# Narrower clears of the value pads, the decayed rows' pads cleared on VectorE alone, and new instruction orders in a fused linear-attention and gated feed-forward kernel

## The chip, the cores and the metric

The kernel runs on one core of one Trainium2 chip. The metric is the device time of one execution in microseconds (us); lower is better. Before the change the median of three runs is 193.56 us (193.5 to 193.87). The engines are TensorE (PE, with PEld for its weight loads), VectorE (DVE), ScalarE (ACT), GpSimd (POOL) and SyncE (SP). Loads and stores are issued from the instruction streams of SP, ACT and POOL, in the order of each stream.

## The reference

```python
# q, k, v, f_logit: (4, 8, 768, 48) = batch, heads, sequence, head size
f = 1.0 / (1.0 + np.exp(-f_logit))
for t in range(S):
    state = f[:, :, t, :, None] * state + np.einsum('bhd,bhe->bhde', k[:, :, t], v[:, :, t])
    y[:, :, t] = np.einsum('bhd,bhde->bhe', q[:, :, t], state)
x = y.transpose(0, 2, 1, 3).reshape(B * S, H * D)          # 3072 x 384
out = (np.maximum(x @ w_gate, 0.0) * (x @ w_val)) @ w_out   # 384 -> 1536 -> 384
```

A recurrence with a decay for every head and key column gives 3072 rows of 384 values; a gated feed-forward network follows.

## The kernel before

**The work.** The sequence is cut into chunks of 128 positions: 6 chunks times 4 batches give 24 blocks. Inside a block the recurrence becomes matrix products: cumulated logarithms of the decay turn into two factors, one on k and one on q (the decayed rows, tile `hats`); scores of k against q are masked and multiplied with v, and a carried state adds the past. The first 16 blocks (chunks 0 and 1) are worked two at a time as a unit of 256 positions, the rest one by one. Four blocks make one feed-forward group of 512 rows. TensorE does the matrix products of both halves, so the attention of later chunks and the feed-forward groups of earlier ones are interleaved.

**Names of operations.** The code records every operation under a short name, with chunk and block: `f`, `k`, `q`, `v` loads are `Lk0.2` (chunk 0, blocks 2 and 3), weight loads `wg0+2` (gate weights, columns 0 and 1 of 12; also `wv`, `wo`), stores `S00`. For block 0.1 the steps are
- `ef`, `ln`: ACT, exponential and logarithm of the forget logits (lines 478, 481), one pair for two blocks
- `cum01`: PE, cumulated sums (lines 494, 498; 503 and 506 in later chunks)
- `ek01`, `eq01`: ACT, exponentials of them (lines 516, 518); `dc01`: the decay of the state
- `hk01`, `hq01`: the decayed rows, k or q times an exponential (line 540 if on POOL, 541 if on DVE); both inputs and the output are in SBUF
- `tk01`, `tq01`: PE transposes of the decayed rows (line 552); `ck01`, `cq01`: their copies out of PSUM (556 DVE, 557 ACT). In chunks 2 to 5 a DMA transpose does both (line 560)
- `v01`: the cast copy of v into the padded tile `vpad` (570 POOL, 571 DVE, 572 ACT)
- `s00`: PE scores of a unit (line 650; later 584); `m000` and so on: DVE masks (657, later 592), four for a unit
- `y00`, `kv00`, `yi01`: PE, values times scores, state products, products with the old state (672, 695, 708; later 745, 756, 772); `st`, `ss`, `sd`: the state's update (450, 454, 456)
- `x01`: copy of the block's output as feed-forward input (line 597)

The feed-forward steps are `g` and `u` (gate and value products, line 792), `r` (relu, 797 ACT or 798 DVE), `p` (product, line 800, DVE), `o` (output product, line 813), `d` (copy out, 819 ACT or 820 DVE). In group 0 the first four columns are done for blocks 0 and 1 and for blocks 2 and 3 apart: `g00.2` and `g02.3` are such halves, of 256 rows instead of 512.

**Who orders it.** Nothing is scheduled when the kernel is built. `ORDER` lists for each engine the numbers of its operations in order, `BANKS` gives the PSUM bank of each product in PE's order, and `HELD` adds waits: `57: 58` makes load 57 wait for the landing of load 58. `lay_out` turns these lists into streams; `waits` puts in the semaphore waits that reads and writes ask for. A negative number in PE's list, such as `~7512`, is a row of idle-time fillers: 7 products of zeros with 512 columns (line 877).

**Pads.** A head is 48 wide. In `hats` every head has 64 columns, the last 16 zero. In `vpad` a pair of heads takes 112 columns: 48 values, 16 pad, 48 values. Products that read 32 columns at a time read the pad too (columns 32 to 63 and 48 to 79 of a pair). `fill` records such a clear as a memset.

```python
    for i in range(NH):       # 6 buffers of hats
        fill("DVE" if i < 3 else "POOL", f"hats{i}", hats[:, i, :, :, D:64], 0.0, 256, -14 + i)
    for i in range(NV):       # 6 buffers of vpad
        fill("POOL", f"vpad{i}", vpad[i][:], 0.0, VW, -8 + i)
```

Of the kernel before, what the change touches and what calls it, by code (L numbers as in the profile page):

```python
# [24 lines left out]
        45, ~60100, 76, 87, ~4512, 84, ~3512, 92, 82, 103, ~2512, 94, 123, 112, 97, ~7512, 120, ~2512, 130, 102, 128, 106,  # L25
        118, 139, 158, 133, 154, 232, 243, ~3512, 150, 152, 146, 138, 279, 268, 142, 156, 160, 148, 174, 176, 170, 172, 186,
# [13 lines left out]
    ],  # L40
    "ACT": [
# [8 lines left out]
    ],  # L50
    "DVE": [
# [25 lines left out]
}  # L77

HELD = {
    51: 53, 57: 58, 59: 63, 63: 58, 65: 69, 67: 71, 70: 50, 71: 60, 72: 54, 517: 68,  # L80
}

BANKS = [
# [158 lines left out]
def bass_hgrn2_outer__then__ffn_reglu_kernel(  # L242
# [10 lines left out]
    B, H, S, D = q.shape  # L253
# [6 lines left out]
    NP = H // 2  # L260
# [4 lines left out]
    VW, SW = NP * VSTEP, NP * SSTEP  # L265
# [7 lines left out]
    hats = sb("hats", [128, NH, 2, H, 64], BF16)  # L273
# [86 lines left out]
    for i in range(NH):  # L360
        fill("DVE" if i < 3 else "POOL", f"hats{i}", hats[:, i, :, :, D:64], 0.0, 256, -14 + i)
    for i in range(NV):
        fill("POOL", f"vpad{i}", vpad[i][:], 0.0, VW, -8 + i)
# [579 lines left out]
```

## Time and profile before

| what | value |
|---|---|
| median of three runs | 193.56 us |
| the profiled execution, its own time | 193.41 us |
| its span | 191.7 us |
| PE busy | 186.0 us, 97% of the span |
| DVE busy | 146.7 us, 77% |
| ACT busy | 83.4 us, 44% |
| POOL busy | 60.0 us, 31% |
| granted TensorE clock over the span | 1.00 |

The span runs from the first to the last instruction of one execution; its own time is 1.71 us more. Busy time is the union of an engine's instructions. The instructions of an engine overlap a little: the next one starts before the record of the one ahead ends. So the steps from start to start are shorter than the durations, and in a merged row of a timeline (a start, a length, a count) the length divided by the count is the step.

### The profile page before, as it was taken

What the parts mean: (1) busy time and instruction counts of PE and PEld (TensorE: products, weight loads), DVE (VectorE), ACT (ScalarE), POOL (GpSimd) and SP (SyncE); (2) the same over time, 40 slices, a digit from 0 to 9 for tenths busy, and PEclk for the clock granted to TensorE, in tenths of its full rate; (3) what the DMA queues carried; (4) which work ended last, traced back from release to release, by engine and by line L of the source; (5) the groups of instructions that cost most, each with busy time, mean ns of one, the idle gap of its engine ahead of it and who ended that gap; (6) DMA issues with size and microseconds to landing.
All of it is one profiled execution on the core that took longest, in us unless ns stands there. A gap on an engine that the chain in (4) does not pass through costs nothing.

```text
span 191.7 us, 4882 instructions
## 1 busy us (share of the span) xinstructions
PE 186.0 (97%) x2006; PEld 109.7 (57%) x2006; DVE 146.7 (77%) x264; ACT 83.4 (44%) x183; POOL 60.0 (31%) x92
## 2 busy tenths in 40 slices
PE   7899999999999999999999999999999999999994
PEld 7555675565645556655455755556555565555553
DVE  4469946999768989879986789996888947677331
ACT  2776963520387780472213996513351220222211
POOL 8899320201055820368200283911180000000000
DMA  5999999999989999899999999993239010000413
GB/s 149 325 285 261 206 208 278 204 225 279 241 185 193 225 212 208 160 187 255 204 162 220 238 203 236 176 202 79 64 120 180 20 41 3 2 0 0 164 44 123
DMA packets 110311, 32.44 MB, mean 169 GB/s; under 512 B 103504, under 2 KB 110032, under 8 KB 110288
## 3 DMA queue, kind: packets, MB, share of 16 engines
q1 hardware_dynamic: 95120, 25.44, 62.4%
q0 software_dynamic: 3776, 3.54, 11.4%
q10 hardware_dynamic: 11392, 3.15, 7.4%
q8 instruction: 16, 0.26, 0.6%
q14 instruction: 7, 0.06, 0.1%
HBM read 25.95 MB, written 4.72 MB: 160 GB/s over the span
## 4 chain that ended last, share of the span: by engine, by line
PE 75%; DMA 10%; DVE 5%; ACT 5%; issue 1%; POOL 1%; SPq 1%; ACTq 0%
PE ps L792 40%; PE ps L813 24%; DMA f_in<-in_f_logit_dram 7%; DMA wg<-in_moe_w_gate_dram 3%; PE ps L584 2%; DVE gT L800 2%; DVE hats L541 2%; PE ps L745 1%; PE ps L672 1%; PE ps L503 1%; POOL hats L540 1%; ACT f_in L478 1%; ACT expo L518 1%; PE ps L756 1%; ACT bneg L481 1%
## 5 line engine op out<-in xcount | busy, mean ns | idle before, releaser
L800 DVE TENSOR_TENSOR gT<-relu,ps 128x512 bf16<-128x512 bf16 (+1 forms) x76 | 48.5, 654 | 15.4 <-PE ps L792 11.4
L792 PE MATMUL ps<-xT,wg 128*128 128x512 bf16 (+1 forms) x228 | 57.8, 368 | 0.1
L792 PE MATMUL ps<-xT,wv 128*128 128x512 bf16 (+1 forms) x228 | 57.5, 368 | 0.0
L813 PE MATMUL ps<-wo,gT 128*128 128x384 bf16 (+2 forms) x300 | 51.9, 320 | 0.2 <-DVE gT L800 0.2
L797 ACT ACTIVATE relu<-ps 128x512 bf16<-128x512 f32 (+1 forms) x39 | 21.8, 565 | 46.2 <-PE ps L792 26.6
L813 PEld LDWEIGHTS ps<-wo,gT 128*128 128x128 bf16 x300 | 27.1, 98 | 18.4 <-DVE gT L800 1.2
L792 PEld LDWEIGHTS ps<-xT,wv 128*128 128x128 bf16 x228 | 23.6, 108 | 19.7 <-ACT expo L518 0.3
L792 PEld LDWEIGHTS ps<-xT,wg 128*128 128x128 bf16 x228 | 23.3, 108 | 19.1 <-DMA wg<-in_moe_w_gate_dram 0.6
L798 DVE TENSOR_SCALAR relu<-ps 128x512 bf16<-128x512 f32 (+1 forms) x37 | 24.8, 673 | 5.4 <-PE ps L792 4.4
L570 POOL CAST vpad<-v_in 128x384 bf16<-128x384 f32 x14 | 7.5, 550 | 43.6 <-PE ps L745 22.4
L592 DVE TENSOR_TENSOR ptm<-ps,tri 128x512 bf16<-128x512 f32 x32 | 19.9, 680 | 1.3 <-PE ps L584 1.3
L540 POOL TENSOR_TENSOR hats<-q_in,expo 128x384 bf16<-128x384 f32 x14 | 14.5, 1045 | 9.5 <-ACT expo L518 8.7
L478 ACT ACTIVATE f_in<-f_in 128x768 f32<-128x768 f32 x12 | 10.1, 845 | 14.1 <-DMA f_in<-in_f_logit_dram 14.0
L540 POOL TENSOR_TENSOR hats<-k_in,expo 128x384 bf16<-128x384 f32 x13 | 13.8, 1071 | 7.0 <-ACT expo L516 3.8
L456 POOL TENSOR_TENSOR st<-ssum,dec 128x384 bf16<-128x384 f32 x11 | 9.7, 878 | 16.1 <-DVE ssum L454 16.1
L518 ACT ACTIVATE expo<-ps 128x384 f32<-128x384 f32 x24 | 11.7, 492 | 4.2 <-PE ps L503 2.9
L597 ACT ACTIVATE xT<-ps 128x384 bf16<-128x384 f32 x10 | 5.4, 548 | 16.9 <-PE ps L672 8.3
L516 ACT ACTIVATE expo<-ps 128x384 f32<-128x384 f32 x24 | 11.6, 493 | 1.1 <-PE ps L494 0.6
L819 ACT ACTIVATE osb<-ps 128x384 f32<-128x384 f32 (+1 forms) x15 | 7.3, 483 | 10.3 <-PE ps L813 9.8
L657 DVE TENSOR_TENSOR ptm<-ps,tmask 128x512 bf16<-128x512 f32 x16 | 10.2, 681 | 1.2 <-PE ps L650 1.1
L877 PE MATMUL ps<-zeros 128*128 128x100 bf16 (+1 forms) x81 | 10.6, 307 | 0.0
L481 ACT ACTIVATE bneg<-f_in 128x768 bf16<-128x768 f32 x12 | 10.1, 842 | 0.2
(78 smaller groups left out, 169.8 us busy)
## 6 DMA issues: line engine op xcount, KB each, us to landing
out_dram<-osb SPq DMA_DIRECT2D x23, 192.0 KB, 2.4
f_in<-in_f_logit_dram SPq DMA_DIRECT2D x11, 384.0 KB, 5.9
k_in<-in_k_dram SPq DMA_DIRECT2D x11, 384.0 KB, 5.7
q_in<-in_q_dram SPq DMA_DIRECT2D x10, 384.0 KB, 5.7
v_in<-in_v_dram SPq DMA_DIRECT2D x8, 384.0 KB, 5.1
v_in<-in_v_dram ACTq DMA_DIRECT2D x4, 384.0 KB, 6.4
q_in<-in_q_dram ACTq DMA_DIRECT2D x2, 384.0 KB, 6.5
wg<-in_moe_w_gate_dram POOLq DMA_DIRECT2D x2, 384.0 KB, 8.8
```

The lines of the kernel that those rows point to most:

```text
L478: add(f"ef{c}{b0}", by("ACT", lambda: sc.activation(raw, raw, AF.Exp, scale=-1.0), act_(n)), keys, keys, key=P)
L481: add(f"ln{c}{b0}", by("ACT", lambda: sc.activation(bo, fl, AF.Ln, bias=1.0), act_(n)), keys + [f"bneg{bi}"], [f"bn{bi}_{x % 2}" for x in ...
L516: add(f"ek{c}{b}", by("ACT", lambda: sc.activation(ex[:, 1, :], bc.ap[:, 0:HD], AF.Exp, scale=1.0), act_(HD)), [bc], [f"expk{ei}"], key=P + 1)
L518: add(f"eq{c}{b}", by("ACT", lambda: sc.activation(ex[:, 0, :], bc.ap[:, 0:HD], AF.Exp, scale=-1.0), act_(HD)), [bc], [f"expq{ei}"], key=P ...
L540: return {**by("POOL", lambda: gp.tensor_tensor(o, i_, e_, ALU.mult), pool_(HD)), **by("DVE", lambda: ve.tensor_tensor(o, i_, e_, ALU.mult ...
L592: add(f"m{c}{b}{j}", by("DVE", lambda b=b, j=j, mi=mi: ve.tensor_tensor(ptm[mi][:, j, :, :], s[b, j].ap[:, :].rearrange("p (n t) -> p n t" ...
L792: z = te.matmul(bank.ap[:, 0:n], wt[:, kt, w_cols(j)], xT[xi][:, kt, n0:n1], start=(kt == 0), stop=(kt == NK - 1))
L797: add(f"r{c}{b0}.{j}", {**by("ACT", lambda: sc.activation(rdst, gate.ap[:, 0:n], AF.Relu), act_(n)), **by("DVE", lambda: ve.tensor_scalar_ ...
L798: **by("DVE", lambda: ve.tensor_scalar_max(rdst, gate.ap[:, 0:n], 0.0), dve_(n))}, [gate], [f"relu{ri}"], key=P)
L800: add(f"p{c}{b0}.{j}", by("DVE", lambda: ve.tensor_tensor(gT[gi][:, j, n0:n1], rdst, val.ap[:, 0:n], ALU.mult), dve_(n)), [val, f"relu{ri} ...
L813: z = te.matmul(o.ap[:, 0:e1 - e0], gT[gi][:, j, b * C:(b + 1) * C], wo[:, j, e0:e1], start=(j == 0), stop=(j == NJ - 1))
L877: te.matmul((op.opens[0].ap if op.opens else banks[7])[:, 0:fill % 1000], zeros[:, 0:128], zeros[:, 0:fill % 1000], start=True, stop=True, ...
```

## The change

The two clears read now:

```diff
     for i in range(NH):
-        fill("DVE" if i < 3 else "POOL", f"hats{i}", hats[:, i, :, :, D:64], 0.0, 256, -14 + i)
+        fill("DVE", f"hats{i}", hats[:, i, :, :, D:64], 0.0, 256, -14 + i)
     for i in range(NV):
-        fill("POOL", f"vpad{i}", vpad[i][:], 0.0, VW, -8 + i)
+
+        fill("POOL", f"vpad{i}", vpad[i][:].rearrange("p (n e) -> p n e", n=NP)[:, :, D:64], 0.0, 64, -8 + i)
```

A clear of `vpad` covers 64 columns instead of 448, and the three clears of `hats` that were on POOL are on DVE. All lists of `ORDER`, all of `BANKS`, and `HELD` are new:

```diff
 ORDER = {
     "PE": [
-        45, ~60100, 76, 87, ~4512, 84, ~3512, 92, 82, 103, ~2512, 94, 123, 112, 97, ~7512, 120, ~2512, 130, 102, 128, 106,
+        45, ~60100, 87, 76, ~7512, 94, ~2512, 84, 92, 82, 103, ~2512, 97, 112, 123, ~7512, 120, 130, 118, ~1512, 102, 128,
...
 HELD = {
-    51: 53, 57: 58, 59: 63, 63: 58, 65: 69, 67: 71, 70: 50, 71: 60, 72: 54, 517: 68,
+    57: 53, 59: 62, 63: 58, 65: 63, 66: 51, 67: 71, 70: 50, 71: 60, 806: 72,
 }
```

The same lists by name, from the first product after the opening fillers to the first gate product of blocks 2 and 3 (F4 is a row of four fillers):

```
PE before:  cum00 cum01 F4 tq00 F3 tk01 tk00 kv00 F2 tq01 cum03 cum02 s00 F7 tq02 F2 tq03 y00 tk03 yi01 tk02 kv02
            g00.3 s02 g00.2 cum10 cum11 F3 g00.1 u00.1 g00.0 y02 cum13 cum12 yi03 u00.2 u00.3 u00.0 g02.3
PE after:   cum01 cum00 F7 tq01 F2 tq00 tk01 tk00 kv00 F2 s00 cum02 cum03 F7 tq02 tq03 tk02 F1 y00 tk03 kv02 yi01
            s02 g00.2 g00.3 F1 g00.0 g00.1 u00.1 cum10 cum11 u00.3 y02 F2 yi03 u00.2 u00.0 g02.3
ACT before: ef00 ln00 eq00 dc00 ek01 eq01 ek00 ef02 ck01 ln02 ek03 v03 eq02 eq03 dc02 ek02 cq03 x00 ef10 ln10
ACT after:  ef00 ln00 v01 ek01 eq01 ek00 eq00 dc00 cq01 ef02 ck01 ln02 v02 eq02 eq03 ek02 dc02 ek03 cq02 cq03 x01 ef10
DVE before: (clears) v01 v00 hq00 cq00 hk00 ck00 st00 ss10 cq01 4 masks cq02 hk03 hk02 ck03 x01 ck02 st01
DVE after:  (clears) v00 hk01 hk00 cq00 ck00 st00 ss10 m000 m010 m001 hq03 hk02 m011 hk03 ck02 x00 ck03 st01
POOL before:(clears) wg2+2 a clear hk01 hq01 wo0+2 wv0+2 sd10 v02 hq02 hq03 wg0+2 wv2+2 wg4+4 wv4+4 wv8+4 wg8+4
POOL after: (clears) wg2+2 2 clears hq01 hq00 wo0+2 wv0+2 wg0+2 v03 sd10 hq02 wv2+2 wg4+4 wv4+4 wv8+4 wg8+4
SP before:  Lf0.0 Lq0.0 Lf0.2 Lv0.2 Lk0.2 Lf1.0 Lf1.2 Lq1.2 Lk1.0 Lq1.0 Lk1.2 Lk3.2 Lv2.2 Lq2.2 Lk2.0
SP after:   Lf0.0 Lq0.0 Lf0.2 Lv0.2 Lk0.2 Lf1.0 Lf1.2 Lq1.2 Lk1.0 Lq1.0 Lk1.2 Lq2.2 Lq2.0 Lf4.0 Lv2.2 Lf2.0
```

Holds before, by name: `wg0+2` waits for `Lk0.2`, `wv2+2` for `Lf1.0`, `Lk1.0` for `wv4+4`, `Lk1.2` for `wv8+4`, `Lk3.2` for `wg8+4`. After: `wg0+2` waits for none, `wv2+2` for `Lk0.2`, `Lq1.2` for `wg0+2`, `Lk1.0` for `wg4+4`, `Lk1.2` for `wv4+4`. `Lk3.2` has none any more, nor has `wo4+4` (it waited for `Lq0.2`), and `Lq5.2` waits for `wo4+4`; `wv4+4`, `wo0+2`, `wo2+2` and `Lv1.2` wait for what they waited for.

Where the feed-forward output of group 0 begins, the orders read:

```
PE before:  tk12 u00.8 tk11 tk10 tq13 o02.0 s12 o03.0 o03.4 o02.4 o00.0 o00.4 s10 o00.8 o03.8 y12
PE after:   tk10 u00.8 tk12 o02.0 o03.0 s12 o00.0 o02.4 o03.4 o03.8 s10 o00.4 o00.8 y12
DVE before: p00.8 ck10 cq13 ck11 r00.11 p00.11 4 masks
DVE after:  p00.9 p00.11 cq13 p00.10 ck12 p00.8 cq11 4 masks
POOL before: wo2+2 wo4+4 wo8+4 v12          POOL after: wo2+2 wo4+4 hk13 wo8+4 v12
```

Of the eight copies `ck`, `cq` of chunk 1 five are on DVE before and three after; `hk13` goes from DVE to POOL, and of its `v` copies three are on DVE before and none after.

Over the whole kernel these steps change engines (numbers of operations):

| step | before | after |
|---|---|---|
| `hk`, `hq` | 21 DVE, 27 POOL | 30 DVE, 18 POOL |
| `sd` | 5 DVE, 11 POOL | 8 DVE, 8 POOL |
| `v` | 6 DVE, 14 POOL, 4 ACT | 5 DVE, 9 POOL, 10 ACT |
| `ck`, `cq` | 11 DVE, 5 ACT | 7 DVE, 9 ACT |
| `r` | 37 DVE, 39 ACT | 34 DVE, 42 ACT |

Of chunks 3 to 5 alone, `hk` and `hq` on DVE go from 7 to 12 and `sd` on DVE from 2 to 4. PE has the same products in both, and 22 long fillers instead of 21.

More of the change, by code (lines that the diff above doesn't have):

```diff
@@ L24 @@
     "PE": [
-        45, ~60100, 76, 87, ~4512, 84, ~3512, 92, 82, 103, ~2512, 94, 123, 112, 97, ~7512, 120, ~2512, 130, 102, 128, 106,
-        118, 139, 158, 133, 154, 232, 243, ~3512, 150, 152, 146, 138, 279, 268, 142, 156, 160, 148, 174, 176, 170, 172, 186,
[13 rows of a table removed]
+        45, ~60100, 87, 76, ~7512, 94, ~2512, 84, 92, 82, 103, ~2512, 97, 112, 123, ~7512, 120, 130, 118, ~1512, 102, 128,
+        139, 106, 133, 154, 158, ~1512, 146, 150, 152, 232, 243, 160, 138, ~2512, 142, 156, 148, 174, 166, 168, 170, 172,
[13 rows of a table added]
     ],
     "ACT": [
[8 rows of a table removed]
[8 rows of a table added]
     ],
     "DVE": [
[12 rows of a table removed]
[12 rows of a table added]
     ],
     "POOL": [
[4 rows of a table removed]
[3 rows of a table added]
     ],
     "SP": [
[4 rows of a table removed]
[4 rows of a table added]
     ],
```

99 rows, old and new, of tables (BANKS, ORDER) are left out of this document.

## The prediction

> **What bounds the kernel now.** First the head, the engines' busy time and the fillers' row of the page.
>
> ```profile
> span 191.7 us, 4882 instructions
> PE 186.0 (97%) x2006; PEld 109.7 (57%) x2006; DVE 146.7 (77%) x264; ACT 83.4 (44%) x183; POOL 60.0 (31%) x92
> L877 PE MATMUL ps<-zeros 128*128 128x100 bf16 (+1 forms) x81 | 10.6, 307 | 0.0
> ```
>
> PE is busy for 186.0 of 191.7 us, but 10.6 of these are products of zeros. The other 175.4 us are the same products after the change. What an order can win is the rest: 16.3 us of idle and filler time, of which some 7 lie ahead of the first real product and some 2 behind the last. Where they lie shows the chain that ended last; here two early pieces (start, length, what) and its last.
>
> ```profile
> 14.26 1.90 POOL hats L540 x2
> 16.17 5.73 DMA wg<-in_moe_w_gate_dram
> ...
> 189.05 0.38 ACT osb L819
> ```
>
> The start is bound by a detour: POOL works off two decayed rows, and only then issues the load of gate columns 0 and 1, which PE awaits at 21.94. The timeline of the start has the steps (start, length, instruction).
>
> ```profile
> 1.34 0.72 ACTq L406 DMA_DIRECT2D k_in<-in_k_dram  x1
> 7.02 0.48 PE L494 MATMUL ps<-bneg,tsum 128*128 128x384 bf16 x2 [0.64 <-ACT bneg L481]
> 7.72 0.49 ACT L518 ACTIVATE expo<-ps 128x384 f32<-128x384 f32 x1 [0.85 <-PE ps L498]
> 8.87 0.48 ACT L518 ACTIVATE expo<-ps 128x384 f32<-128x384 f32 x1
> 9.24 0.50 ACT L516 ACTIVATE expo<-ps 128x384 f32<-128x384 f32 x1
> 10.01 1.32 POOL L540 TENSOR_TENSOR hats<-q_in,expo 128x384 bf16<-128x384 f32 x1
> 11.48 0.83 ACT L481 ACTIVATE bneg<-f_in 128x768 bf16<-128x768 f32 x1
> 13.30 0.64 PE L650 MATMUL ps<-qkT 48*64 48x128 bf16 x32
> 13.99 2.48 DVE L657 TENSOR_TENSOR ptm<-ps,tmask 128x512 bf16<-128x512 f32 x4 [1.10 <-PE ps L650]
> 16.72 1.01 DVE L541 TENSOR_TENSOR hats<-k_in,expo 128x384 bf16<-128x384 f32 x2
> 19.18 0.64 PE L650 MATMUL ps<-qkT 48*64 48x128 bf16 x32
> 21.02 0.81 PE L877 MATMUL ps<-zeros 128*128 128x512 bf16 x3
> 21.94 0.12 PEld L792 LDWEIGHTS ps<-xT,wg 128*128 128x128 bf16 x2 [0.60 <-DMA wg<-in_moe_w_gate_dram]
> 23.91 0.82 PE L494 MATMUL ps<-bneg,tsum 128*128 128x384 bf16 x4
> 24.84 0.18 PEld L708 LDWEIGHTS ps<-qkT,st 128*32 128x32 bf16 x12
> 26.12 0.49 PE L792 MATMUL ps<-xT,wg 128*128 128x256 bf16 x3
> ```
>
> I take g02.3, at 26.12, as the mark: behind it PE hardly idles. The windows show it (length, then PE, PEld, DVE, ACT, POOL busy).
>
> ```profile
> 36.00:54.00 18.00, 17.79 (x343) 10.85 (x341) 16.60 (x33) 4.57 (x9) 1.98 (x4) 1.00 1.15 234
> ...
> 86.00:101.00 15.00, 15.00 (x81) 7.98 (x80) 13.44 (x21) 2.77 (x5) 5.67 (x7) 1.00 1.14 210
> 101.00:109.00 8.00, 8.00 (x171) 5.09 (x172) 5.61 (x10) 4.94 (x11) 0.51 (x1) 1.00 1.16 229
> 109.00:126.00 17.00, 16.79 (x126) 8.84 (x113) 15.86 (x24) 12.28 (x32) 11.37 (x12) 1.00 1.11 211
> ```
>
> So three places count: the start, the stretch from 36 to 54 where DVE works 92% of the time, and the stretch to 126, again with DVE at 93%.
>
> **The clears.** Rows of the groups by shape:
>
> ```profile
> L328 POOL MEMSET vpad<- 128x448 bf16 x6 | 2.8, 482 | 0.0
> L328 POOL MEMSET hats<- 128x256 bf16 x3 | 1.0, 321 | 0.0
> L328 DVE MEMSET hats<- 128x128 uint32 x3 | 0.5, 165 | 0.1
> ```
>
> POOL loses three clears of 0.321 and about two thirds of 2.8 us (64 columns cannot cost over a clear of 256, 0.321, so at least 6 x 0.16 = 1.0 goes), DVE gets 3 x 0.165 = 0.5. Both end before the first exponential at 7.72 lets either go on, so this is worth nothing on the path; without that cover DVE would lose the 0.5. What it does is to let POOL issue wg2+2 earlier, a load that no row waits for.
>
> **The start, step by step.** cum01 goes first and has no narrow products behind its two wide ones, so ek01 starts at 7.02 + 0.48 + 0.04 = 7.54 instead of eq00 at 7.72. Four exponentials at the step of 9.24 - 8.87 = 0.37 to 0.39 end at 9.2. Now hk01, hk00 go to DVE while hq01, hq00 go to POOL. What that costs shows this place, and the landing of k from the table of DMA issues (7.1 us from 1.34, so 8.4):
>
> ```profile
> k_in<-in_k_dram ACTq DMA_DIRECT2D x1, 384.0 KB, 7.1
> 110.33 1.00 POOL L540 TENSOR_TENSOR hats<-q_in,expo 128x384 bf16<-128x384 f32 x1 [0.45 <-ACT expo L518]
> 110.67 1.08 DVE L541 TENSOR_TENSOR hats<-k_in,expo 128x384 bf16<-128x384 f32 x1 [0.69 <-ACT expo L516]
> 111.44 1.17 POOL L540 TENSOR_TENSOR hats<-k_in,expo 128x384 bf16<-128x384 f32 x1
> ```
>
> DVE's row, 0.5 to 0.55 alone (16.72: two in 1.01), ends at 111.75, 0.42 behind the end of POOL's at 111.33: it waited for it. And POOL's, 1.00 alone, takes 1.32 when DVE is ahead (10.01). Both start here at about 8.45, so either DVE is first (hk01 to 9.0, hq01 to 9.75, hk00 to 10.2, hq00 to 11.05) or POOL is (hq01 to 9.45, hk01 to 9.9, hq00 to 10.75, hk00 to 11.15). All four rows are ready at 11.1, before at 10.01 + 1.32 = 11.33.
>
> The Trainium skill (SBUF — State Buffer, section "Who interferes with whom") says that a VectorE instruction with two SBUF inputs contends with a GpSimd one that reads SBUF, and that the first to issue blocks the other. By it the later transposes come at 11.1, as above; if such pairs ran freely, DVE would be ready at 9.6 and POOL at 10.5, and the start would gain some 0.5 more.
>
> From there: tq00 at 10.8 to 11.1, then on DVE the copies cq00 and ck00 (0.4 each in the same timeline, and three transposes between) to 12.05 or 12.35, and s00 at 12.4 to 12.7, 0.6 to 0.9 before 13.30. The price: ef02 and ln02 stand behind cq01 on ACT now, which waits for hq01. ln02 ends near 12.75 to 13.05, before at 12.31, and the second four exponentials, in the same queue, end near 15.7 instead of 15.3. That is covered: DVE has three masks to do first, from 13.05 to 14.85 at 2.48 / 4 = 0.6 each. hq03 waits for POOL's hq02 to 15.25 and ends at 15.7; hk02, m011, hk03 (steps 0.5, 0.6, 0.5) end at 17.25, before at 17.73. ck02, x00, ck03 and st01 follow, so s02 starts at 18.55 to 18.85, 0.3 to 0.6 before 19.18. If that DVE row of eleven instructions slips, s02 slips with it.
>
> wg0+2 is issued behind wv0+2, near 12.1, not at 16.17, and lands by 5.73 more at 18: ahead of g00.0 at 20. The 0.9 us from 21.02 to 21.94 (fillers and the wait) go; one filler (0.22) and two (0.43) stand elsewhere. What is late next is DVE: with s02 done at 19.2, ss11, three masks, r00.1 and the fourth mask at 0.6 each let y02 start at about 22.2; y02 and yi03 with two fillers end at 23.6, x03 takes 0.6 more, and g02.3 starts near 24.4 to 24.7. It owes cum12 and cum13 then, 24.84 - 23.91 = 0.93. So the mark is at 25.3 to 25.6 against 26.12: **a gain of 0.5 to 0.8, taken as 0.65.**
>
> **The output of group 0 (36 to 54).** Here s12 waited for a copy on DVE:
>
> ```profile
> 41.00 0.81 PE L813 MATMUL ps<-wo,gT 128*128 128x384 bf16 x4
> 42.02 0.64 PE L650 MATMUL ps<-qkT 48*64 48x128 bf16 x32 [0.21 <-DVE qkT L556]
> 42.60 3.42 PE L813 MATMUL ps<-wo,gT 128*128 128x384 bf16 x20
> ```
>
> Twenty output products take 3.42 behind that, so four take 0.68; o02.0, at 41.00, holds PE for 1.02: 0.34 lost. After the change two copies, hk13 and three v copies leave DVE in this stretch, to ACT with 4.57 us of work in 18 and to POOL with 1.98, and o03.0 stands between o02.0 and s12, 0.68 more of cover. I take the 0.34 as won; bounds 0 and 0.9 (smaller gaps of that stretch too). The price: hk13 stands ahead of wo8+4 on POOL, and waits for ek13, which by the same walk ends near 34.7. So that load goes out near 36 and lands by 6 to 8 more at 42 to 44. Its first user, o03.8, follows o02.0 by five output products and a score block, 5 x 0.68 + 0.6 = 4.0, at 44 to 45. This margin is rival 3.
>
> **The rest.** Nine more hats and three more state decays are 12 x 0.5 = 6 us for DVE (half of the 1.01 at 16.72); three relus of 0.6 (a mask's step), four copies and a v copy of no more than 0.5 go, together 4. Against the net of 2 stands that POOL, with 12 two-input operations fewer, holds DVE up less:
>
> ```profile
> L541 DVE TENSOR_TENSOR hats<-q_in,expo 128x384 bf16<-128x384 f32 x10 | 8.6, 858 | 1.3 <-ACT expo L518 1.3
> L541 DVE TENSOR_TENSOR hats<-k_in,expo 128x384 bf16<-128x384 f32 x11 | 6.8, 632 | 0.7 <-ACT expo L516 0.7
> ```
>
> Over 0.55 each that is 3.1 + 0.9 = 4.0 us of blocked time. I take the two as even: 0, bounds -0.5 and +2 (below). At the end nothing is moved on the path: the last output product, a copy of 0.38, a store.
>
> Sum, against the profiled execution of 193.41 (its span of 191.7 and 1.71 around it): -0.65 - 0.34 + 0 = -1.0, so 192.4. The median is 0.15 over that execution, so 192.55; as the bounds reach further up than down, I say 192.7.
>
> **The rivals.** (1) DVE becomes the bound between 86 and 126, slower than before. There it is busy for 34.9 of 40 us, 5.1 free. Five more hats and two more decays of chunks 3 to 5 fall there: 7 x 0.5 = 3.5 us alone, 7 x 1.2 = 8.4 if each meets a POOL row. It decides from a mean of 0.73 on: beyond that PE waits for p and r to free banks. At 1.0 to 1.2 PE waits 1.9 to 3.3, less the 1.0 won ahead: 194.5 to 195.9, I say 194.8. For it: 93% in the last stretch, and the 1.08 above. Against it: POOL has fewer partners to meet.
> (2) The gain of the start is given back: hk01 starts late, weights come late, or the gaps of some 0.1 us that a just-met wait leaves on PE move to other places. 193.5, no change; also what follows if only the clears did anything.
> (3) A load is late: wo8+4 behind hk13, or Lf2.0, which stands behind Lq2.0 and Lf4.0 on SP now. One wait of 1 to 2 us less 0.65: about 194.2. For it: a load of half that size took 5.73 (wg0+2); against it: f2.0's exponential comes only behind the first feed-forward products of group 1, behind 53.
>
> **How the numbers follow.** Forecast 192.7: 0.45, own range 192.2 to 193.1. A larger gain (small gaps go too), 191.9: 0.05. No change, 193.5: 0.18. Rival 1: 0.20. Rival 3: 0.12. What a measurement can tell from no change is 0.2%, 0.39 us: faster 0.50, same 0.18, slower 0.32. The range leaves out the worst of rival 1 and the best of the gains: 191.9 to 194.7.
>
> **What would show it.** Right: ek01 near 7.54, scores at line 650 near 12.5 and 18.7, wg0+2 issued near 12, no DMA releaser at the first gate products, g02.3 ahead of cum12 near 24.5, s12 without a wait for a copy. Wrong: line 541 rows of 1.2 in the start's first pair only on DVE and s02 not earlier than 19.18; DVE over 95% between 86 and 126 with PE waits on line 800; a DMA releaser ahead of o03.8 or of line 478 in chunk 2.

## The result and the profile after

| | before | after |
|---|---|---|
| median, us | 193.65 (20 executions) | 194.31 (20 executions) |
| lowest and highest, us | 193.35 and 194.88 | 193.47 and 195.47 |
| profiled execution, us | 193.41 | 194.56 |
| its span, us | 191.7 | 192.8 |

The ratio after to before is 1.0034, 95% interval 1.0022 to 1.0047: slower by a third of a per cent, where 192.7, 0.4% faster, was forecast. The medians of the experiments are of 4 to 12 executions each and come with the kernel before on the same chip, whose median was 193.55 to 193.65 in every comparison. The trace of e1 comes from an execution of 240.38 us at a granted clock of 0.757 and is not used below.

The head of the page, the row of the fillers, and pieces of the chain that ended last (start, length, what), of the kernel after:

```profile
span 192.8 us, 4863 instructions
PE 185.0 (96%) x1989; PEld 109.4 (57%) x2007; DVE 148.9 (77%) x272; ACT 90.0 (47%) x195; POOL 43.1 (22%) x72
L877 PE MATMUL ps<-zeros 128*128 128x100 bf16 (+1 forms) x78 | 9.6, 296 | 0.3 <-issue 0.2
1.94 9.51 DMA f_in<-in_f_logit_dram
13.08 8.12 DMA wg<-in_moe_w_gate_dram
65.98 0.85 ACT bneg L481
```

185.0 less 9.6 is 175.4 us of real products, as before; the span has 17.4 us of idle and filler time in place of 16.3. The start hangs on other things than before. The load f0.2, issued at 1.94, lands at 11.45; the gate load of columns 0 and 1 follows it and takes 8.12. Later a piece of ACT (`ln22`) is on the chain, which no part of the forecast had.

The timeline of the start, before and then after (start, length, instruction, idle time ahead of it and what ended it). First two rows of before that the prediction did not need:

```profile
6.73 0.95 POOL L431 DMA_DIRECT2D wg<-in_moe_w_gate_dram  x1
10.25 0.84 ACT L478 ACTIVATE f_in<-f_in 128x768 f32<-128x768 f32 x1 [0.52 <-DMA f_in<-in_f_logit_dram]
```

```profile
4.24 0.94 POOL L431 DMA_DIRECT2D wg<-in_moe_w_gate_dram  x1
8.32 2.27 POOL L540 TENSOR_TENSOR hats<-q_in,expo 128x384 bf16<-128x384 f32 x2 [2.94 <-ACT expo L518]
11.47 0.84 ACT L478 ACTIVATE f_in<-f_in 128x768 f32<-128x768 f32 x1 [1.06 <-DMA f_in<-in_f_logit_dram]
11.75 0.59 POOL L431 DMA_DIRECT2D wo<-in_moe_w_out_dram  x1 [1.16 <-DMA f_in<-in_f_logit_dram]
12.95 0.64 PE L650 MATMUL ps<-qkT 48*64 48x128 bf16 x32 [0.47 <-ACT qkT L557]
13.08 0.78 POOL L431 DMA_DIRECT2D wg<-in_moe_w_gate_dram  x1
13.64 1.89 DVE L657 TENSOR_TENSOR ptm<-ps,tmask 128x512 bf16<-128x512 f32 x3 [0.50 <-PE ps L650]
19.40 0.64 PE L650 MATMUL ps<-qkT 48*64 48x128 bf16 x32
21.24 0.83 PE L792 MATMUL ps<-xT,wg 128*128 128x256 bf16 x6 [0.21 <-DMA wg<-in_moe_w_gate_dram]
26.04 0.83 PE L792 MATMUL ps<-xT,wg 128*128 128x256 bf16 x6
```

POOL is done with its short clears earlier and issues `wg2+2` at 4.24 instead of 6.73. `ef02`, at line 478, then waits for f0.2 until 11.47 instead of 10.25, and so does POOL's `wo0+2`, which is held for f0.2, with `wv0+2` and `wg0+2` behind it; wg0+2 lands at 21.20, and g00.0 waits 0.21 for it. `ck01` and `ln02` stand behind `ef02` on ACT: s00 waits for that copy, and s02 is at 19.40, not at 18.55 to 18.85.

Four products have exactly the same products ahead of them in both orders, so their starts (of the first weight load, from the trace) can be compared directly. "After, again" is a second profiled execution of the same kernel, the last row one of the experiments:

| kernel (profiled execution, us) | tq12 | y12 | o01.8 | o53.4b | o01.8 to o53.4b |
|---|---|---|---|---|---|
| before (193.41) | 33.71 | 47.93 | 52.88 | 187.42 | 134.54 |
| after (194.56) | 34.49 | 48.32 | 53.35 | 188.61 | 135.26 |
| after, again (193.56) | 34.33 | 48.16 | 52.96 | 187.58 | 134.62 |
| wg2+2 and Lv2.0 moved (193.22) | 33.93 | 47.76 | 52.56 | 187.17 | 134.61 |

The start (to tq12) lost 0.62 to 0.78 where 0.65 was to be won. From tq12 to y12, which holds the output of group 0, all three new executions take 13.83 against 14.22: 0.39 won, 0.34 forecast. The rest takes 134.62 against 134.54 in one execution of after, and 0.72 more than before in the other: there the wait for `ln22` is in it. So the profiled execution lost 0.78 - 0.39 + 0.08 + 0.72 = 1.19 at o53.4b, and the second 0.16. The loss has a fixed part in the start and parts that come and go with the execution.

### The profile page after: what moved, and what is told of

Same layout as the page of the kernel before. It is cut to its first block, busy times and chain, and to the rows that moved or that the text cites. A ratio compares the mean times of both kernels' runs of the same rounds, so it can differ in the third digit from the quotient of the medians.

```text
span 192.8 us, 4863 instructions
## 1 busy us (share of the span) xinstructions
PE 185.0 (96%) x1989; PEld 109.4 (57%) x2007; DVE 148.9 (77%) x272; ACT 90.0 (47%) x195; POOL 43.1 (22%) x72
## 4 chain that ended last, share of the span: by engine, by line
PE 82%; DMA 9%; DVE 2%; ACT 2%; issue 1%; POOL 1%; SPq 1%; DVEq 0%
PE ps L792 44%; PE ps L813 25%; DMA f_in<-in_f_logit_dram 5%; DMA wg<-in_moe_w_gate_dram 4%; PE ps L584 2%; PE ps L745 2%; DVE gT L800 1%; PE ps L503 1%; PE ps L672 1%; PE ps L772 1%; DVE relu L798 1%; PE ps L552 1%; PE ps L756 1%; PE ps L752 1%; PE ps L494 1%
## 5 line engine op out<-in xcount | busy, mean ns | idle before, releaser
L792 PE MATMUL ps<-xT,wg 128*128 128x512 bf16 (+1 forms) x223 | 56.6, 368 | 0.7 <-DMA wg<-in_moe_w_gate_dram 0.2
L792 PE MATMUL ps<-xT,wv 128*128 128x512 bf16 (+1 forms) x219 | 56.3, 367 | 0.5
L797 ACT ACTIVATE relu<-ps 128x512 bf16<-128x512 f32 (+1 forms) x42 | 23.9, 575 | 47.5 <-PE ps L792 30.6
L798 DVE TENSOR_SCALAR relu<-ps 128x512 bf16<-128x512 f32 (+1 forms) x34 | 22.3, 662 | 2.1 <-PE ps L792 1.6
L540 POOL TENSOR_TENSOR hats<-q_in,expo 128x384 bf16<-128x384 f32 x11 | 11.9, 1085 | 20.1 <-DMA q_in<-in_q_dram 12.1
L819 ACT ACTIVATE osb<-ps 128x384 f32<-128x384 f32 (+2 forms) x15 | 7.1, 471 | 18.5 <-PE ps L813 16.6
L456 POOL TENSOR_TENSOR st<-ssum,dec 128x384 bf16<-128x384 f32 x8 | 7.0, 876 | 35.3 <-DVE ssum L454 21.4
L541 DVE TENSOR_TENSOR hats<-k_in,expo 128x384 bf16<-128x384 f32 x17 | 12.1, 722 | 3.5 <-DMA k_in<-in_k_dram 2.5
L540 POOL TENSOR_TENSOR hats<-k_in,expo 128x384 bf16<-128x384 f32 x7 | 7.6, 1093 | 27.7 <-ACT expo L516 27.7
L516 ACT ACTIVATE expo<-ps 128x384 f32<-128x384 f32 x24 | 11.1, 491 | 4.1 <-PE ps L503 2.1
L657 DVE TENSOR_TENSOR ptm<-ps,tmask 128x512 bf16<-128x512 f32 x16 | 10.1, 683 | 1.8 <-PE ps L650 1.8
L541 DVE TENSOR_TENSOR hats<-q_in,expo 128x384 bf16<-128x384 f32 x13 | 8.9, 698 | 3.0 <-ACT expo L518 2.9
L481 ACT ACTIVATE bneg<-f_in 128x768 bf16<-128x768 f32 x12 | 10.1, 840 | 0.2
```

Source lines behind the costliest of these rows:

```text
L481: add(f"ln{c}{b0}", by("ACT", lambda: sc.activation(bo, fl, AF.Ln, bias=1.0), act_(n)), keys + [f"bneg{bi}"], [f"bn{bi}_{x % 2}" for x in ...
L516: add(f"ek{c}{b}", by("ACT", lambda: sc.activation(ex[:, 1, :], bc.ap[:, 0:HD], AF.Exp, scale=1.0), act_(HD)), [bc], [f"expk{ei}"], key=P + 1)
L540: return {**by("POOL", lambda: gp.tensor_tensor(o, i_, e_, ALU.mult), pool_(HD)), **by("DVE", lambda: ve.tensor_tensor(o, i_, e_, ALU.mult ...
L541: **by("DVE", lambda: ve.tensor_tensor(o, i_, e_, ALU.mult), dve_(HD))}
L657: add(f"m{c}{b2[i]}{j}", by("DVE", lambda i=i, j=j, mask=mask: ve.tensor_tensor(ptm[mi[i]][:, j, :, :], s[j, i].ap[:, :].rearrange("p (n t ...
L792: z = te.matmul(bank.ap[:, 0:n], wt[:, kt, w_cols(j)], xT[xi][:, kt, n0:n1], start=(kt == 0), stop=(kt == NK - 1))
```

## The experiments

Theory 1: the shorter clears let POOL issue wg2+2 earlier, and this load takes DMA time from f0.2. Theory 2: the new orders cost the start by themselves. Theory 3: Lv2.0, issued by ACT in the middle of its work, holds `ef22` and `ln22`. Theories 5, 6 and 7 came up on the way; no theory bears the number 4.

**The load alone, in the order of before.** All clears as before, one load moved on POOL:

```diff
- stsum1 stmask0 mhats3 sident mones mvpad3 mhats5 mtmask1 mvpad5 stmask1 wg2+2 mvpad4 hk01
+ stsum1 wg2+2 stmask0 mhats3 sident mones mvpad3 mhats5 mtmask1 mvpad5 stmask1 mvpad4 hk01
```

> The kernel before, with one load moved: POOL issues wg2+2 behind stsum1, near 4.4 instead of 6.7; all clears are the long ones. Theory 1: f0.2 lands near 11.4 instead of 10.2, wo0+2 goes out 0.2 to 0.5 later, ln02 and s02 come up to 0.8 later, and the time is 0.3 to 0.8 above before: 193.9 to 194.4. Theory 2: no change, 193.6, since nothing of the orders is touched.

Measured: 195.06, ratio 1.0087 (1.0060 to 1.0114). Its timeline:

```profile
4.35 0.95 POOL L431 DMA_DIRECT2D wg<-in_moe_w_gate_dram  x1
11.46 0.84 ACT L478 ACTIVATE f_in<-f_in 128x768 f32<-128x768 f32 x1 [1.87 <-DMA f_in<-in_f_logit_dram]
13.58 0.82 PE L494 MATMUL ps<-bneg,tsum 128*128 128x384 bf16 x4 [1.57 <-ACT bneg L481]
14.51 0.64 PE L650 MATMUL ps<-qkT 48*64 48x128 bf16 x32
15.08 3.08 PE L877 MATMUL ps<-zeros 128*128 128x512 bf16 x7
21.77 0.64 PE L650 MATMUL ps<-qkT 48*64 48x128 bf16 x32
```

Issued 2.4 us earlier, the load moves the start of `ef02` by 1.2, from 10.25 to 11.46, and in this order, where s00 stands behind cum02, s00 by 1.2 as well, from 13.30 to 14.51. No order is changed otherwise, so that much is shown. s02 comes 2.6 later, but the other 1.4 are not the load's wait itself: the granted clock, 1.00 there in before, is 0.80 from 14 to 16, 0.50 from 16 to 18 and 0.84 from 18 to 20, and the seven fillers take 3.08 us instead of this row of before:

```profile
13.87 1.68 PE L877 MATMUL ps<-zeros 128*128 128x512 bf16 x7
```

The low clock follows PE's idle 1.57 us ahead of 13.58; that the one comes of the other was not tested. Three of the six executions have a mean granted clock of 0.991 to 0.998 and took 195.32 to 196.11. The three at 0.999 or 1.00 took 194.31 to 194.80, 0.7 to 1.2 above before; this is the price at full clock, and the 1.5 of the median holds some of the clock. The Trainium skill (DMA: Bandwidth & Descriptors, section "Queues, rings and completion order") says that each DMA engine goes round the queues that have work, packet by packet. The traces fit this: f0.2 went out at 1.94, wg2+2 at 4.35 here and at 4.24 in the kernel after, on another queue, and in both kernels the two land within 0.1 us of each other, at 11.4; with wg2+2 behind hq00 f0.2 lands at 10.0 to 10.1 (e14, e15, e18, e20).

**The clears alone, in the order of before.** Only the diff's line for `vpad`; all orders and holds as before.

> The kernel before, with only the clears of vpad made short, every order and every hold as before. Theory 1: wg2+2 goes out near 4.5 to 5.5 instead of 6.7, f0.2 lands 0.5 to 1.2 later than 10.2, ln02 and s02 start later by as much, and the time is 0.3 to 0.8 above before: 193.9 to 194.4. Theory 2, and the prediction (clears worth nothing on the path): no change, 193.6.

Measured: 193.73, ratio 1.0001 (0.9991 to 1.0011). Its rows:

```profile
5.60 0.95 POOL L431 DMA_DIRECT2D wg<-in_moe_w_gate_dram  x1
10.44 0.84 ACT L478 ACTIVATE f_in<-f_in 128x768 f32<-128x768 f32 x1 [0.50 <-DMA f_in<-in_f_logit_dram]
```

wg2+2 goes out at 5.60 only, since other clears of the old order stay ahead of it, and f0.2 lands at 10.4. So the clears alone cost nothing; it is clears and POOL's new order together that bring the load to 4.24.

**The load behind hq00, or last, in the order after.**

```diff
 e1:
- sl1 sl0 wg2+2 mones mvpad3 hq01 hq00 wo0+2 wv0+2 wg0+2 v03 sd10
+ sl1 sl0 mones mvpad3 hq01 hq00 wg2+2 wo0+2 wv0+2 wg0+2 v03 sd10
 e7:
- sl1 sl0 wg2+2 mones mvpad3 hq01 hq00 wo0+2 wv0+2 wg0+2 v03 sd10
+ sl1 sl0 mones mvpad3 hq01 hq00 wo0+2 wv0+2 wg0+2 wg2+2 v03 sd10
```

> The kernel after, with one load moved: POOL issues wg2+2 behind hq00 instead of ahead of mones. Theory 1 (the shorter clears let POOL issue wg2+2 at 4.2 us instead of 6.7; it shares the DMA engines with f0.2 and q0.2, so that f0.2 lands at 11.45 instead of 10.23, and ef02, wo0+2 and wg0+2 wait for it): f0.2 lands near 10.2, ef02 starts near 10.5, wg0+2 goes out near 12.1 instead of 13.1, s02 starts at 18.5 to 18.9 instead of 19.4, and the time is 193.5 to 193.8, that is 0.5 to 0.8 below after. Theory 2 (the new orders of the start cost it): f0.2 may land earlier, but s02 stays near 19.4 and the time within 0.2 of after, 194.3.

> The kernel after, with one load moved: POOL issues wg2+2 behind wg0+2 instead of ahead of mones; so it lies ahead of neither wo0+2, wv0+2 nor wg0+2, and its issue of 0.95 us holds none of them. Theory 1: f0.2 lands near 10.3 and q0.2 near 10.9, wo0+2 goes out near 10.7, wg0+2 near 12, ln02 ends near 13.0, s02 starts at 18.5 to 18.9, and the time is 193.3 to 193.7. Theory 2 (the orders of the start cost it by themselves): f0.2 lands early and s02 still starts at 19.2 or later; the time stays above 193.9.

Measured: 193.54 for the first, ratio 1.0009 (0.9986 to 1.0033); 194.77 for the second, 1.0057 (1.0042 to 1.0072). In the second f0.2 is on time (`ef02` at 10.44, s00 at 12.54), but g00.2, the first gate product, needs the very columns of wg2+2, waits 0.62 for them at 20.47, and the gain is gone. "Last" was my mistake: the load is needed at 20, and must only stay clear of f0.2. The trace is of an execution of 193.89; why the median is 0.9 above that, it does not show.

**Full clears with the order after.** e3 puts the old line for `vpad` back; e10 does so with wg2+2 behind wg0+2.

> The kernel after, with the full clears of vpad of the kernel before put back, orders as after. Theory 1: POOL's clears hold wg2+2 back again to 6 us or later, f0.2 lands near 10.2 to 10.6, and the time is 0.3 to 0.8 below after: 193.5 to 194.0. The longer clears may hold hq01 back if they end behind 8.3; then the gain is smaller. Theory 2: no change or slower, 194.3 or more.

> The kernel after, with wg2+2 behind wg0+2 and the full clears of vpad put back. The clears then stand ahead of no load that goes out before 10.6; POOL ends them near 6.5, ahead of hq01 at 8.3. The prediction's step (clears worth nothing on the path by themselves) and theory 1: the same time as with wg2+2 behind wg0+2 and short clears, within 0.15. If the short clears are worth something by themselves: slower than that by 0.2 or more.

Measured: 194.04, ratio 1.0033 (1.0005 to 1.0061), and 194.53, 1.0052 (1.0033 to 1.0071). The first stands between the theories and says little. Its trace is of an execution of 196.31 (a second took 196.20) that went another way from the first load on: f0.0 landed at 6.19 instead of 4.96, PE sat idle from 6 to 8 us, and the granted clock was 0.51 from 8 to 10 and 0.64 from 10 to 12. wg2+2 went out at 5.88 there, and f0.2 still landed at 11.34, not at 10.2 to 10.6 as theory 1 had it. The second is e7's time within its scatter, and its tq12 is at 34.25 against 34.29: where no early load stands behind the clears, their length is worth nothing.

**Lv2.0.**

```diff
 ACT:
- Lq5.2 r10.8 Lv2.0 r10.9 ef22 ln22
+ Lq5.2 r10.8 r10.9 ef22 ln22
 SP:
- S02 S00 Lv3.2 Lk2.2 S01 Lf2.2
+ S02 S00 Lv3.2 Lv2.0 Lk2.2 S01 Lf2.2
```

> The kernel after, with one load moved: Lv2.0 is issued by SP ahead of Lk2.2 instead of by ACT ahead of r10.9. Theory 3 (that issue holds ACT's queue for 2.5 us at 62, so that r10.9, ef22 and ln22 come late and PE waits at cum22): no wait of cum22 at 67, PE gains 0.4 to 0.8 there, and the time is 193.6 to 194.0. Rival (another instruction of ACT or the bank of r10.9 sets it, or the gain is given back in the stretch to 126): the wait stays or the time stays at 194.3.

Measured: 193.81, ratio 1.0014 (0.9997 to 1.0032). The place in the timeline of the kernel after:

```profile
62.06 2.51 ACTq L411 DMA_DIRECT2D v_in<-in_v_dram  x1
64.62 0.60 ACT L797 ACTIVATE relu<-ps 128x512 bf16<-128x512 f32 x1 [1.97 <-PE ps L792]
65.11 0.84 ACT L478 ACTIVATE f_in<-f_in 128x768 f32<-128x768 f32 x1
65.98 0.84 ACT L481 ACTIVATE bneg<-f_in 128x768 bf16<-128x768 f32 x1
66.97 0.32 PE L503 MATMUL ps<-bneg,tri 128*128 128x384 bf16 x1 [0.44 <-ACT bneg L481]
```

and with the load on SP:

```profile
63.70 0.84 ACT L478 ACTIVATE f_in<-f_in 128x768 f32<-128x768 f32 x1 [0.77 <-DMA f_in<-in_f_logit_dram]
64.58 0.84 ACT L481 ACTIVATE bneg<-f_in 128x768 bf16<-128x768 f32 x1
66.02 0.33 PE L503 MATMUL ps<-bneg,tri 128*128 128x384 bf16 x1
```

The releaser named for the relu at 64.62 had long been done; what it waited for is the issue ahead of it, 2.51 us in ACT's queue. Without it, `ef22` waits for f2.2 alone, and cum22 for nothing.

**f2.2.** In e4 `ef22` just meets f2.2, which SP now issues behind the store S01; that could as well be the cause (theory 7). e16 moves only this load, e17 moves it with Lv2.0:

```diff
 SP:
- Lf2.0 S02 S00 Lv3.2 Lk2.2 S01 Lf2.2
+ Lf2.0 Lf2.2 S02 S00 Lv3.2 Lk2.2 S01
```

> The kernel after, with one load moved: SP issues Lf2.2 right behind Lf2.0, ahead of S02, S00, Lv3.2, Lk2.2 and S01, near 51 us instead of 58.7. Theory 7 (f2.2 stands behind the store S01, lands at 62 to 64 and is just met by ef22, so every delay of the loads ends in the time): f2.2 lands before 58; if that alone sets cum22, its wait of 0.4 goes and the time is 193.6 to 193.9. Theory 3 alone (ACT's issue of Lv2.0 holds ACT from 62 to 64.6, and ef22 stands behind it in any case): the wait at cum22 stays and the median is within 0.2 of after, 194.3, perhaps with less scatter.

> The kernel after, with Lf2.2 right behind Lf2.0 on SP and Lv2.0 on SP ahead of Lk2.2. Theory 7 with theory 3: no wait at cum22, f2.2 long landed when ef22 starts; median 193.4 to 193.7, no execution above 194.4. If f2.2 has nothing to do with the scatter: median 193.8 and executions up to 195 as with Lv2.0 moved alone.

Measured: 194.41, ratio 1.0054 (1.0033 to 1.0075), and 193.79, 1.0022 (1.0006 to 1.0038). In e16 f2.2 landed at 55.5, and nothing was won:

```profile
61.92 2.39 ACTq L411 DMA_DIRECT2D v_in<-in_v_dram  x1
66.71 0.32 PE L503 MATMUL ps<-bneg,tri 128*128 128x384 bf16 x1 [0.32 <-ACT bneg L481]
```

So theory 3 stands and theory 7 falls as the cause of this wait. Over the traces: the time from o01.8 to o53.4b is 134.61 to 134.63 in six kernels with Lv2.0 on SP (e4, e5, e15, e17, e18, e21; 134.73 in e20), and between 134.62 (twice) and 135.80 in eight profiled executions with it on ACT (after twice, e3, e7, e10, e12, e13, e16): 0 to 1.2 us, and in the order of the issue's length. Issues of 1.63 and 1.86 us cost nothing, 2.26 to 2.51 cost 0.37 to 0.64, 2.88 and 3.07 cost 0.97 and 1.18. One kernel with Lv2.0 on SP stands apart, e14 with 136.22, where f2.2 itself is late (below). The medians agree in part: the move reads -0.62 from e16 to e17 and -0.86 from e7 to e5, each pair on one chip, but +0.34 from e1 to e15, on two chips.

**Both causes.** e5 is e7 with Lv2.0 on SP, e15 is e1 with Lv2.0 on SP.

> The kernel after with both moves: wg2+2 behind wg0+2 on POOL, Lv2.0 on SP ahead of Lk2.2. If the two causes add, 0.6 to 0.8 for the first and 0.5 for the second, below 194.3: 192.9 to 193.3, faster than before as well. If what is won at the start is given back in front of the first wait behind it, as the stall at cum22 would do: 193.5 or more.

> The kernel after with two moves: wg2+2 behind hq00 (so that it lands ahead of its first product g00.2, unlike behind wg0+2) and Lv2.0 on SP ahead of Lk2.2. Theories 1 and 3 add: f0.2 lands near 10.3, no DMA wait at g00.2, no wait at cum22, 193.0 to 193.4. If the start gives nothing (s02 stays at 19.2 to 19.4 behind POOL's queue): the same as with Lv2.0 on SP alone, 193.7 to 193.9.

Measured: 193.91, ratio 1.0025 (1.0005 to 1.0046), and 193.88, 1.0020 (0.9999 to 1.0041). e5 has the wait for wg2+2 at g00.2 as e7 has. e15's profiled execution took 193.22, the shortest of those profiled; its start:

```profile
10.26 0.83 ACT L478 ACTIVATE f_in<-f_in 128x768 f32<-128x768 f32 x1
10.49 0.94 POOL L431 DMA_DIRECT2D wg<-in_moe_w_gate_dram  x1
12.36 0.64 PE L650 MATMUL ps<-qkT 48*64 48x128 bf16 x32
13.05 1.89 DVE L657 TENSOR_TENSOR ptm<-ps,tmask 128x512 bf16<-128x512 f32 x3
14.79 0.99 POOL L540 TENSOR_TENSOR hats<-q_in,expo 128x384 bf16<-128x384 f32 x1
14.86 1.35 DVE L541 TENSOR_TENSOR hats<-q_in,expo 128x384 bf16<-128x384 f32 x1
19.06 0.64 PE L650 MATMUL ps<-qkT 48*64 48x128 bf16 x32
25.48 0.83 PE L792 MATMUL ps<-xT,wg 128*128 128x256 bf16 x6
```

With f0.2 on time s00 and the masks are where the forecast had them (12.4 to 12.7, 13.05). From hq03 on it is late again: it runs beside POOL's hq02 and takes 1.35. At tq12 the three kernels with wg2+2 behind hq00 and POOL's order otherwise that of after (e15, e18, e20) stand at 33.93 to 34.07, mean 34.02; those with it early at 34.15 to 34.58 (after twice, e4, e12, e16, e17, e21), mean 34.38. So the early load costs the new order 0.36 us there, and the new start, without it, still 0.31 against before's 33.71 (one trace; e2, with the same order, has 33.91): theory 2 has a part too. Whole times show the 0.36 in part only: the medians move by -0.40 (e19 to e1), -0.38 (e17 to e18), -0.05 (e21 to e20) and +0.07 (e4 to e15), the first and the last of these pairs on two chips, and each sure to some 0.2 to 0.5 us only.

**POOL's queue, and v1.0.** Theory 6 puts that rest on hq02's place behind four load issues, `v03` and `sd10`. Theory 5 puts the spread of the executions on v1.0, which now lands shortly ahead of y10. e13 and e12 test one each; e14 joins both with e15.

```diff
 e13, POOL:
- wg0+2 v03 sd10 hq02 wv2+2
+ wg0+2 hq02 v03 sd10 wv2+2
 e12, ACT and SP (and the hold of Lv1.2 on wo2+2 goes):
- ck10 Lv1.2 Lv1.0 Lk2.0
+ ck10 Lk2.0
- Lk1.2 Lq2.2 Lq2.0 Lf4.0
+ Lk1.2 Lq2.2 Lv1.2 Lv1.0 Lq2.0 Lf4.0
```

> The kernel after, with POOL's order changed in one place: hq02 ahead of v03 and sd10. Theory 6 (the second pair of decayed rows is late because POOL does four load issues, v03 and sd10 ahead of hq02, so that hq02 still runs when DVE starts hq03, which it then blocks): hq02 starts near 14.4 instead of 15.12, hq03 takes 0.55 to 0.9 instead of 1.1 to 1.3 and ends near 15.8, hk03 ends near 17.3, s02 starts at 18.7 to 19.0 instead of 19.4, and the time is 0.2 to 0.5 below after. Rival (ln02, late by f0.2, sets the second exponentials and so the rows): hq02 waits for eq02 near 14.6 to 15, s02 gains less than 0.2, the time stays.

> The kernel after, with two loads moved: Lv1.2 and Lv1.0 are issued by SP behind Lq2.2 and ahead of Lq2.0 and Lf4.0, near 33 us, instead of by ACT near 41 behind them; the hold of Lv1.2 on wo2+2 goes. Theory 5 (SP's loads Lq2.0 and Lf4.0 go out ahead of these two, so that v1.0 lands at 48.6 to 50.8, where y10 needs it cast at 49.9; the executions in which it lands behind 49.3 lose up to 1.5 us): v1.0 lands before 44, y10 at 50.0 waits for no cast, the median is 0.2 to 0.5 below after, 193.8 to 194.1, and the executions above 194.8 are gone or rare. Rival (the scatter comes from elsewhere): the same median and the same scatter, 193.5 to 195.5; or wo8+4 or q2.0, now later, makes a wait of its own at o03.8 or in chunk 2.

> The kernel after with four moves: wg2+2 behind hq00, Lv2.0 on SP ahead of Lk2.2, Lv1.2 and Lv1.0 on SP behind Lq2.2, hq02 ahead of v03 and sd10. If the four causes are the whole loss: s02 at 18.5 to 18.9, no wait at y10 and cum22, 192.4 to 192.9, so faster than before by 0.4 to 0.6%, as the prediction had it. If something else sets the time (the wait for masks in front of y02, the stretch 80 to 85): 193.2 or more.

Measured: 195.34, ratio 1.0090 (1.0077 to 1.0103); 194.41, 1.0038 (1.0023 to 1.0053); 195.44, 1.0092 (1.0077 to 1.0107). All three miss. In e13 hq02 waits for its exponential until 14.83, as the rival had it, and s02 stays at 19.40. Even with f0.2 on time, in e14, s02 gains only 0.05 against e15: hq03 ends at 15.85 instead of 16.21, but hk02 behind it then takes 0.85 beside `v03` and `sd10`. So theory 6 falls. And in e13 wv2+2 goes out behind all of them, at 17.65 instead of 16.07, so the loads up to Lq2.2 land later (wg8+4 at 33.09 instead of 31.76). In the time its profiled execution lost 1.02 against after between y12 and o01.8, where PE stopped in y10 (last section). In e14, which has all four moves, f2.2 lands at 66.0 instead of e15's 63.1, and PE waits for it at cum22; which of the moves makes it late is open:

```profile
66.03 0.84 ACT L478 ACTIVATE f_in<-f_in 128x768 f32<-128x768 f32 x1 [2.84 <-DMA f_in<-in_f_logit_dram]
67.89 0.32 PE L503 MATMUL ps<-bneg,tri 128*128 128x384 bf16 x1 [1.45 <-ACT bneg L481]
```

e12's median stays, as its rival said. That v1.0 can cost is shown by e10's profiled execution (195.03), where v1.0 landed at 50.8 and the cast held y10:

```profile
50.81 0.51 POOL L570 CAST vpad<-v_in 128x384 bf16<-128x384 f32 x1 [2.60 <-DMA v_in<-in_v_dram]
51.47 0.78 PE L672 MATMUL ps<-ptm,vpad 64*32 64x128 bf16 x64 [1.19 <-POOL vpad L570]
```

**Three and four moves, and after again.** e18 is e15 with Lf2.2 behind Lf2.0. e21 is e17 with v1.2 and v1.0 moved as in e12; e20 is e18 with the same. e19 is the kernel after, unchanged.

> The kernel after, with three moves: wg2+2 behind hq00, Lv2.0 on SP ahead of Lk2.2, Lf2.2 right behind Lf2.0. The start wins 0.4 to 0.6 (g02.3 near 25.5), cum22 has no wait, and the scatter is gone: median 193.0 to 193.3, below before by 0.15 to 0.3%, no execution above 194. Rival (the scatter has another source, such as v1.0 at y10): median 193.8, executions to 195 as without the third move.

> The kernel after, unchanged. Theories 1, 3 and 7: f0.2 lands near 11.4, f2.2 at 62 or later, a wait at cum22, 194.3 with a scatter of 193.5 to 195.5.

> The kernel after, with Lf2.2 right behind Lf2.0, Lv2.0 on SP ahead of Lk2.2, and Lv1.2 and Lv1.0 on SP behind Lq2.2. Theory 5 (v1.0, just met at y10, makes the executions above 194.4 that are left): v1.0 lands before 46, no wait at y10, median 193.6 to 193.8, no execution above 194.4. Rival: the same 193.8 with executions at 194.5 to 195.3; or f4.0, f2.0 and f2.2, now later by two loads, meet ef40 or ef22 and make it 194 or more.

> The same with wg2+2 behind hq00 as well. If the load moves add: 193.1 to 193.4, no execution above 193.9, below before by 0.1 to 0.3%. If Lv1.2 and Lv1.0 ahead of Lq2.0 and Lf4.0 make another load late: 193.6 or more, above the 193.41 of the three moves.

Measured: e18 193.41, ratio 0.9994 (0.9984 to 1.0005), 193.26 to 194.16; e19 193.94, 1.0029 (1.0010 to 1.0048), 193.40 to 195.58; e21 193.75, 1.0014 (0.9995 to 1.0033); e20 193.70, 1.0015 (0.9992 to 1.0038). e18 is the best version of the new order: 0.5 below after on the same chip (0.9 below the 194.31 of the result). Against before no difference can be measured, so no version here beats before.

The spread is not settled. Of 32 executions of after 13 lie above 194.4, of 148 of before 2, of 12 of e18 none; but e15 has 2 of 12, and e17, e20 and e21, with 3, 3 and 2 of 12, have them still, the last two with v1.0 out of the way. So v1.0 is not the whole cause, and e18's quiet twelve may be luck.

## Why the prediction was wrong

The sum was -0.65 (start) -0.34 (output of group 0) + 0 (rest). In the two profiled executions of the kernel after it came out at +0.62 and +0.78 (to tq12), -0.39 (to y12), and -0.07 and +0.80 (from there to o53.4b). So two terms failed. The start lost where it was to win: 0.36 of that by an early load that was put at nothing, 0.96 by rows of DVE that were sized too short. The rest was put at 0 without the issue of a load on ACT, which costs 0 to 1.2. Point by point:

- **The clears: the early load, put at nothing.** "Both end before the first exponential ... so this is worth nothing on the path" holds (e2, e10). The next sentence doesn't: "What it does is to let POOL issue wg2+2 earlier, a load that no row waits for." No row waits for wg2+2, but rows wait for f0.2, which wg2+2 delays by 1.2 us. The question was not who waits for the moved load, but which loads are in flight when it goes out. Shown by e6 (0.7 to 1.2 us in the old order at full clock) and by the marks of the new order (0.36).
- **ln02 and wg0+2.** "ln02 ends near 12.75 to 13.05" and "wg0+2 is issued ... near 12.1" are both f0.2's landing in disguise: `ef02` and the hold of `wo0+2` wait for it. They came at 13.53 and 13.08; in e7, with the load out of the way, at 12.76 and 12.13. wg0+2's 5.73 us from before's row was no constant either: 8.12 in the kernel after, so it landed at 21.20 and not at 18.
- **The first pair of rows** on DVE and POOL was right: ready at 11.01 against 11.1, and that the two engines hold each other up shows in POOL's 2.27 for two.
- **The second pair, and the masks behind it: the largest miss.** "hq03 waits for POOL's hq02 to 15.25 and ends at 15.7": in e15, with everything ahead on time, hq02 runs 14.79 to 15.78 and hq03 ends at 16.21. I had counted `wg0+2` as moved ahead on POOL, but not the 0.5 to 0.9 us that each of the four load issues, `v03` and `sd10` take there before hq02. Moving hq02 ahead of `v03` and `sd10` doesn't cure it (e14): what was too short is the time that DVE's rows lose to whatever POOL does beside them. Behind s02 the sum is 0.6 short by its own terms: six steps of 0.6 from 19.2 end at 22.8, not at 22.2. In e15 s02 came at 19.06, not at 18.55 to 18.85, and y02 at 23.00. These 0.8 are most of the 0.96 between the gain of 0.65 and the loss of 0.31 at tq12 without the early load.
- **The output of group 0:** right in place and size, 0.39 against 0.34; s12 waits for no copy any more; wo8+4 landed at 44.3, just behind the forecast 42 to 44, and nothing waited for it.
- **The rest: 0.** Right without waits (134.62 against 134.54), and rival 1 is off the table. The window 86 to 126 of the kernel after (length, then PE, PEld, DVE, ACT, POOL busy) has DVE at 92% and PE at 99.6%:

```profile
86.00:126.00 40.00, 39.84 (x368) 22.15 (x370) 36.80 (x62) 19.83 (x45) 13.50 (x15) 1.00 1.00 194
```

- **Rival 3 (a load is late)** had the kind of loss and the wrong load; that its 194.2 lies so near the measured 194.31 is luck. I looked for loads that land late, wo8+4 and Lf2.0. What cost was the issue of Lv2.0, which stood on ACT at 44 before, where ACT had little to do, and stands at 62 now, ahead of `ef22`: 0 to 1.2 us, by e4, e16 and the eight traces with it on ACT. It is not on the list of moved steps in the prediction at all.

## What to carry to other kernels

Where a change lets an engine issue a load earlier, list the loads that are in flight at that moment and what waits for each; a load that nobody waits for can still delay one that sets the path, and the cure is to put it behind the work that needs the other load, but ahead of its own first use. Count DMA issues as work of the engine that makes them, in the sum and in the queue behind them, and put none on an engine ahead of a step that a critical product waits for. An order that just meets many of its waits, as this one does, may spread more from execution to execution (13 of 32 above 194.4 here, against 2 of 148), though why it does is open: judge it by a median over many, not by one trace.

## What the hardware showed beside that

The issue of one 384 KB load on ACT's queue took 0.37 us at 41.01 (Lv1.2) and 2.51 us at 62.06 (Lv2.0) in the kernel after, and 1.6 to 3.1 us for Lv2.0 over the eight traces. So the size does not set it. What does is open: the DMA engines were as busy around the short issue as around the long one (a share of 1.21 from 41 to 42, 1.23 from 62 to 64.6), the two loads cut their 384 KB into pieces of 96 and of 48 values (lines 406 and 411), and SP was issuing loads of its own up to 62.58 and again from 63.06.

In the middle of y10 PE stopped in some executions without any wait of its own. In e13's timeline:

```profile
50.35 0.24 PE L672 MATMUL ps<-ptm,vpad 64*32 64x128 bf16 x6 [0.16 <-DVE osb L820]
51.41 0.68 PE L672 MATMUL ps<-ptm,vpad 64*32 64x128 bf16 x58 [0.81 <-issue]
```

The DMA table of its page has a queue of kind "instruction":

```profile
q8 instruction: 16, 0.26, 0.6%
```

16 packets of 16 KB, from 13.8 us on, 0.26 MB in all. I take them for PE's own instruction stream, since no other engine has as many instructions (2007 weight loads and as many products). The Trainium skill (Runtime: NRT & Kernel Launch, section "Instruction fetch mechanics") says that the sequencer fetches the next 16 KB page by its own DMA queue, at a cost that is mostly hidden. The size agrees. If the fetch makes the stop, it is not hidden here. From the packet times in the trace, the page that was fetched ahead of y10, and the gap behind y10's seventh weight load:

```
kernel   page ends   y10 starts   gap, us   goes on at
e13      49.95       50.32        1.04      51.41
e14      49.05       49.71        0.66      50.39
e17      48.79       50.66        0.28      50.99
after    48.64       50.21        0.21      50.47
e18      48.58       49.77        0.13      49.91
e10      48.50       51.44        0.09      51.57
e3       50.13       51.63        none
e4       48.59       50.07        none
e15      48.26       49.63        none
e19      47.13       50.03        none
```

The gap is always at the same instruction, and the work goes on no sooner than 1.3 us behind the page's end; the long gaps are where y10 starts less than 0.7 us behind it. The delay from the page's end isn't constant, though (1.3 to 2.2 us, and 3.1 in e10), and e15 and e4 start 1.4 and 1.5 behind the page without a gap, where e17 starts 1.9 behind it with one. That the page is the cause is read from this agreement alone; it is not shown, and no experiment moved it. It is a candidate for the part of the spread that is still open.
